# A cross network on one core: column tiles for the main matmuls, a second copy of the tail operand, a new load order, and a last layer with rows on partitions

## The chip, the cores and the metric

The kernel runs on one core of a Trainium2 chip. The metric is the device time of one execution in microseconds, the median of the runs; it was 140.9 us before the change (three runs, 139.42 to 141.42). The profile is one further execution, recorded by the hardware profiler; its span is 139.6 us. The engines are TensorE (PE; its weight loads are PEld), VectorE (DVE), ScalarE (ACT), GpSimd (POOL) and SyncE (SP), whose queue issues most DMAs. "Us" is microseconds everywhere.

## The reference

```
B, F, D, L = 4096, 26, 16, 6
Din = min(F * D, 1024)          # 416
# x0 [4096, 416], ws [6, 416, 416], bs [6, 416], all bf16
def reference(x0, ws, bs):
    x = x0
    for l in range(ws.shape[0]):
        x = x0 * (x @ ws[l] + bs[l]) + x
    return x
```

Six cross layers over 4096 rows of 416 features.

## The kernel before

Since every layer multiplies by `x0` and adds `x`, the state of layer l is x0 times a sum, S, that only grows: S after layer l is S before plus `x @ ws[l]` plus the bias. The kernel therefore keeps S in PSUM, lets TensorE accumulate into it through all six layers, and has another engine form `x = x0 * (S + bias)` from it. The biases are summed once over the layers (`cb_sb`, from a small matmul of a triangle of ones).

The features stand on partitions. The 416 features are three chunks of 128 (`NC = 3`) and a tail of 32 (`DR`). The 4096 rows are four blocks of 1024 columns (`NS = 4`, `SB = 1024`); a block goes through all six layers before the next. The tail of a block is packed: the four groups of 256 rows (`G`) lie on the four quadrants of 32 partitions, so the tail operand `xt_sb` is 128 x 256. PSUM has eight banks of 128 x 512 fp32: six hold S of the three chunks, one half bank (`TAIL`) S of the packed tail, another half (`SPARE`) the tail transposes of the next block.

TensorE runs, for each block and layer, in this order:

- `chunk(m, 0)`: the first half of the columns (512), as 18 matmuls of 128 x 128 weights and 256 columns (L263);
- the tail's rows into the three chunks: 12 matmuls whose contraction is the 32 tail features, tile shape 32 x 128, four row groups side by side (L312). They wait for the tail operand of this layer (`s_xt`) and for the second half's evictions (`s_xb`);
- the tail's outputs: 12 matmuls of 128 x 32 column tiles (L198), and four more with `wc_sb`, a block-diagonal copy of the 32 x 32 corner of the weights, for tail into tail;
- in layer 1, the transposes of the next block's tail (`tail_transposes`);
- `chunk(m, 1)`: the second half, 18 matmuls.

VectorE evicts a half as three 128 x 512 operations (L414): `x = (S + bias) * x0`, in bf16, into `xT_sb`, or into `xo_sb` after the last layer. ScalarE adds the bias to the tail (L457) into `t32_sb`, GpSimd multiplies it by the tail of x0 (L182) into `xt_sb` or, after the last layer, `xot_sb`. The corner copies into `wc_sb` are GpSimd's (L167): the first four after the layer-0 tail weights land, the others after the tail weights of layers 1 to 5 land.

A finished block is stored by SP's queue: three DMA transposes of `xo_sb` into `o_sb` (L129), one of `xot_sb` into `ot_sb` (L133), and, after GpSimd has moved `ot_sb` into the last 32 columns of `o_sb` (L190), one store (L136). GpSimd's part stands in its program behind the layer-1 product of the next block:

```
if l == 1 and s > 0:
    pool.wait_ge(s_ot, 16 * s)
    pool.tensor_copy(out=o_sb[...], in_=ot_sb[...]).then_inc(s_otc, 1)
```

The last block is not transposed by DMA: TensorE transposes it (L350, L364), VectorE and ScalarE copy it out of PSUM, and four stores follow.

At the start, the first 512 rows come in as rows and are transposed on TensorE (L225), the next 512 and the other blocks through transposing DMAs (L111, L121). SP's queue issues, in order: the first rows, weights of layer 0, the tail columns of rows 512 to 1023 (`xtl_sb`, L108), half of the layer-0 tail weights (the other half is ScalarE's queue), the transposing load of the first block's second half, weights of layer 1, tail weights of layers 1 to 5, weights of layers 2 to 5, the tail columns of the other blocks (L119), and the transposing loads of blocks 1 to 3. The order of all engines' programs is written out by hand with semaphores.

## Time and profile before

| What | Value |
|---|---|
| Median of three runs | 140.9 us (139.42 to 141.42) |
| Span of the profiled execution | 139.6 us, mean granted TensorE clock 0.981 |
| Chain that ended last | PE 83%, SP's queue 6%, DMA 5% |
| Main matmuls 128x256 (L263) | 864, 276 and 273 ns each, overlapping |
| Evictions 128x512 (L414) | 143, 744 ns each |
| Tail bias 128x256 (L457), tail product (L182) | 474 ns, 671 ns |
| Corner copies (L167) | 32x32 and 32x160, 201 to 321 ns |
| Output copy of the tail (L190) | 398 ns |
| Transposing stores: three of `xo_sb`, one of `ot_sb` | issued from 43.58, 73.83, 104.09; `ot_sb` from 48.74, 78.95, 108.13, landing 2.4 us after issue |

Rows of the profile give a line of the kernel, the engine, the operation, its output and inputs, shapes, and the mean length of one. [...] "Idle before" is the time the engine stood still ahead of an operation, and what ended it. An issue on SP's queue takes time on SP; the landing is counted from the issue.

### The profile page before, as it was taken

The page shows a single profiled execution, that of the slowest core. Times are in us where ns is not written, and L with a number is a line of the kernel's source. Part 1 is how long each engine was busy: PE and PEld are TensorE (multiplying, and loading weights), DVE is VectorE, ACT ScalarE, POOL GpSimd, SP SyncE. Part 2 cuts the span into 40 slices and gives each one's busy share as a digit, 9 for nine tenths or more (in the row PEclk, how much of TensorE's full clock was granted, in tenths as well). Part 3 has the DMA queues.
Part 4 walks back from the last instruction along what each step waited for, and adds up shares of the span by engine and source line. Part 5 has one row for each costly group of instructions (what it writes and reads, how often), then busy time and mean ns, then how long its engine had stood idle before and what let it go on. Part 6 is the DMA issues. An engine that isn't in the chain of part 4 may idle for free.

```text
span 139.6 us, 3659 instructions
## 1 busy us (share of the span) xinstructions
PE 129.5 (93%) x1638; PEld 102.3 (73%) x1638; DVE 98.5 (71%) x149; ACT 18.0 (13%) x38; POOL 22.3 (16%) x45
## 2 busy tenths in 40 slices
PE   6799389999999999999999999999999999999950
PEld 4677167877877887887787787787788788778730
DVE  0338505977977887897797797798779779779560
ACT  1510110110111021011011021001101101101370
POOL 5023400110110120111011021011011111101500
PEclk9999969999999999999999999999999999999997
DMA  4999799940004947000007934000008461000007
GB/s 132 229 249 315 114 229 227 129 97 5 0 0 39 116 97 249 0 0 5 0 0 43 189 105 161 0 5 0 0 5 159 90 206 38 5 0 0 5 3 244
DMA packets 32939, 12.17 MB, mean 87 GB/s; under 512 B 25238, under 2 KB 32924, under 8 KB 32924
## 3 DMA queue, kind: packets, MB, share of 16 engines
q1 hardware_dynamic: 32272, 11.45, 39.8%
q10 hardware_dynamic: 652, 0.48, 1.0%
q8 instruction: 13, 0.21, 0.7%
q14 instruction: 2, 0.02, 0.0%
HBM read 3.22 MB, written 3.41 MB: 47 GB/s over the span
## 4 chain that ended last, share of the span: by engine, by line
PE 83%; SPq 6%; DMA 5%; issue 1%; ACT 1%
PE ps L263 66%; PE ps L198 9%; PE ps L312 7%; DMA xtl_sb<-in_x_dram 5%; SPq L113 2%; SPq L116 1%; SPq L111 1%; SPq L110 1%; ACT o_sb L464 1%; PE ps L350 0%; SPq L108 0%; ACT o_sb L476 0%; SPq L106 0%; SPq L107 0%; ACT o_sb L469 0%
## 5 line engine op out<-in xcount | busy, mean ns | idle before, releaser
L414 DVE SCALAR_TENSOR_TENSOR xT_sb<-ps,cb_sb,x0T_sb 128x512 bf16<-128x512 f32 x120 | 81.1, 744 | 27.2 <-PE ps L312 24.0
L263 PE MATMUL ps<-xT_sb,w_sb 128*128 128x256 bf16 x720 | 84.4, 276 | 0.0
L263 PEld LDWEIGHTS ps<-xT_sb,w_sb 128*128 128x128 bf16 x720 | 69.7, 99 | 12.4 <-issue 3.6
L182 POOL TENSOR_TENSOR xt_sb<-t_sb,x0t_sb 128x256 bf16<-128x256 f32 x20 | 13.4, 671 | 85.6 <-ACT t_sb L457 85.6
L457 ACT ACTIVATE t_sb<-ps,cb_sb 128x256 f32<-128x256 f32 x24 | 11.4, 474 | 105.5 <-PE ps L198 105.5
L414 DVE SCALAR_TENSOR_TENSOR xo_sb<-ps,cb_sb,x0T_sb 128x512 bf16<-128x512 f32 x23 | 15.6, 744 | 4.5 <-PE ps L312 3.9
L263 PE MATMUL ps<-x0T_sb,w_sb 128*128 128x256 bf16 x144 | 17.1, 273 | 0.0
L263 PEld LDWEIGHTS ps<-x0T_sb,w_sb 128*128 128x128 bf16 x144 | 13.7, 98 | 2.5 <-issue 0.8
L312 PE MATMUL ps<-xt_sb,wt_sb 32*128 32x256 bf16 x240 | 10.1, 271 | 1.2 <-issue 1.2
L198 PE MATMUL ps<-xT_sb,w_sb 128*32 128x256 bf16 x240 | 10.2, 276 | 0.0
L312 PEld LDWEIGHTS ps<-xt_sb,wt_sb 32*128 32x128 bf16 x240 | 4.5, 92 | 5.6 <-issue 5.5
L198 PEld LDWEIGHTS ps<-xT_sb,w_sb 128*32 128x32 bf16 x240 | 4.6, 95 | 4.3 <-issue 4.2
L198 PE MATMUL ps<-xt_sb,wc_sb 128*32 128x256 bf16 x80 | 5.7, 273 | 0.0
L182 POOL TENSOR_TENSOR xot_sb<-t_sb,x0t_sb 128x256 bf16<-128x256 f32 x4 | 2.7, 672 | 13.1 <-ACT t_sb L457 13.1
L205 PE MATMUL ps<-ones_sb 128*128 128x256 bf16 x16 | 3.4, 391 | 1.2 <-POOL ones_sb L149 1.2
L394 DVE COPY x0T_sb<-ps 128x256 bf16<-128x256 bf16 x4 | 1.1, 291 | 4.6 <-PE ps L225 4.4
L205 PEld LDWEIGHTS ps<-ones_sb 128*128 128x128 bf16 x16 | 2.1, 139 | 1.9 <-POOL ones_sb L149 1.2
L167 POOL COPY wc_sb<-wt_sb 32x32 bf16<-32x32 bf16 (+1 forms) x8 | 2.1, 260 | 7.0 <-DMA wt_sb<-in_ws_dram 6.6
L198 PE MATMUL ps<-ident,xtl_sb 128*32 128x128 bf16 x28 | 1.2, 221 | 1.8 <-DMA xtl_sb<-in_x_dram 1.8
L198 PEld LDWEIGHTS ps<-ident,xtl_sb 128*32 128x32 bf16 x28 | 0.7, 96 | 2.1 <-DMA xtl_sb<-in_x_dram 2.1
L198 PEld LDWEIGHTS ps<-xt_sb,wc_sb 128*32 128x32 bf16 x80 | 2.1, 97 | 0.0
L198 PE MATMUL ps<-x0T_sb,w_sb 128*32 128x256 bf16 x48 | 2.0, 276 | 0.0
(35 smaller groups left out, 25.0 us busy)
## 6 DMA issues: line engine op xcount, KB each, us to landing
out_dram<-o_sb SPq DMA_DIRECT2D x3, 832.0 KB, 4.1
w_sb<-in_ws_dram SPq DMA_DIRECT2D x6, 312.0 KB, 6.6
out_dram<-o_sb SPq DMA_DIRECT2D x3, 208.0 KB, 2.3
wt_sb<-in_ws_dram SPq DMA_DIRECT2D x4, 130.0 KB, 4.5
xin_sb<-in_x_dram SPq DMA_DIRECT2D x1, 208.0 KB, 2.8
xin_sb<-in_x_dram ACTq DMA_DIRECT2D x1, 208.0 KB, 3.0
out_dram<-o_sb ACTq DMA_DIRECT2D x1, 208.0 KB, 2.6
xtl_sb<-in_x_dram SPq DMA_DIRECT2D x1, 192.0 KB, 7.6
```

What stands on the lines that cost most here:

```text
L110: sp.dma_start(wt_sb[32 * g:32 * g + 32, 0, :], ws[0, DF:D, :]).then_inc(s_wt[0], 16)
L111: sp.dma_start_transpose(x0T_sb[:, :, H:SB], x0[H:SB, 0:DF]).then_inc(s_x0T[0], 16)
L113: sp.dma_start(w_sb[:, l, :, :], wmain(l)).then_inc(s_w[l], 16)
L116: sp.dma_start(wt_sb[32 * g:32 * g + 32, 1:L, :], ws[1:L, DF:D, :].rearrange("l p n -> p l n")).then_inc(s_wt[1], 16)
L167: pool.tensor_copy(out=wc_sb[p, a:b, p], in_=wt_sb[p, a:b, DF:D]).then_inc(s_wc, 1)
L182: pool.tensor_tensor(out=dst, in0=t32_sb[:, n % 2, :], in1=x0t_sb[:, s, :], op=ALU.mult).then_inc(s_xt, 1)
L198: return pe.matmul(dst, lhsT=lhsT, rhs=rhs, start=start, stop=True, skip_group_check=True, tile_position=(0, 32 * q),)
L205: pe.matmul(ps[:, 7, 0:256], lhsT=ones_sb[:, 0:128], rhs=ones_sb[:, :], start=True, stop=True)
L263: ins = pe.matmul(ps[:, b, c:c + G], lhsT=w_sb[:, l, k, m * 128:(m + 1) * 128], rhs=src[:, k, off + g * G:off + (g + 1) * G], start=l == 0 ...
L312: ins = pe.matmul(ps[:, b, c:c + G], lhsT=wt_sb[p, l, m * 128:(m + 1) * 128], rhs=srct[p, :], start=l == 0 and g >= 2 and i < 2, stop=True ...
L414: dve.scalar_tensor_tensor(out=split(dst), in0=acc_half(c, half), scalar=cb_sb[:, c, l:l + 1], in1=split(x0T_sb[:, c, o:o + H]), op0=ALU.a ...
L457: act.activation(out=t32_sb[:, n % 2, :], in_=TAIL, func=ACTF.Identity, bias=cb_sb[:, NC, l:l + 1],).then_inc(s_ta, 1)
```

## The change

The engine programs are now recorded in one list through a small planner, `Plan.add`: each operation names what it reads, writes and accumulates into, and the waits are derived. The planner does not reorder: every engine runs its operations in the order of the calls. Its GpSimd copies that move data to other partitions (`shifts=True`) wait for the GpSimd operation ahead of them to end.

What differs in the work:

1. **Main matmuls.** Each 128 x 128 x 256 pair becomes four 128 x 32 column tiles of 512 columns, one PSUM bank for each half and chunk (`bank(h, m)`). 
2. **Tail.** The tail operand is held twice: `[:, 0]` as before, `[:, 1]` with neighbouring quadrants swapped (`swap`). Quadrants 0 and 2 then cover 512 columns in one row tile; quadrants 1 and 3 do it in two of 256. The corner, tail into tail, is done among the row tiles (with `wc_sb` in a new layout), and no longer among the column tiles. S of the tail lies in two half banks, so ScalarE's bias becomes two operations of 64 partitions. After GpSimd's product, two of the four swapped quadrants are copied by ScalarE and two by GpSimd; for the tail of x0 of a new block ScalarE copies all four, in layer 1 of the block before, ahead of that layer's bias.
3. **Loads.** See `load_...` below; the rows of the last block (`xr_sb`, 832 KB) are loaded as well. The ones are set by VectorE, and ScalarE runs a dummy activation first.
4. **Store of a block.** `store_block(s)` is called after a block's layers, so that GpSimd's copy (L450) stands directly behind the block's last product, ahead of the next block's first. SP waits chunk by chunk.
5. **Last layer of the last block.** Its output is made with rows on partitions: for each 128 rows, three matmuls of `x` against 416 columns of weights, three that bring in S so far (`sS_sb`, evicted by ScalarE) through the identity, and the tail likewise; VectorE (for two tiles ScalarE and GpSimd) multiplies by `xr_sb`, and five stores follow. The transposes on TensorE at the end are gone.

The core of the diff, with the lines that the prediction speaks of:

```
+        load_rows("sync", 0)
+        load_rows("scalar", 1)
+        load_main(0)
+        load("scalar", bsa_sb[1:L + 1, :], bs[:, :], "bs", [("bs",)])
+        load_transposed(0, H, SB)
+        load("sync", xtl_sb[:, 4:JS, :], x0_v[:, 4:JS, DF:D], "xtl0", [("xtl", 0)])
+        load_tail_weights(0, 1, "wt0")
+        load_main(1)
+        load_tail_weights(1, L, "wt1")
+        load_main(2)
+        load("sync", xtl_sb[:, JS:NJ, :], x0_v[:, JS:NJ, DF:D], "xtl1", [("xtl", 1)])
+        load_main(3)
+        load_main(4)
+        load_main(5)
+        for s in range(1, NS):
+            load_transposed(s, 0, SB)
+        load("sync", xr_sb[:, :, :], x0_v[:, (NS - 1) * JS:NJ, :], "xr", [("xr",)])
...
+        def main(s, l, h, m, k):
+                for q in range(4):
+                    f0 = m * 128 + 32 * q
+                    ins = mm(
+                        pe, ps[quad(q), bank(h, m), :], w_sb[:, l, k, f0:f0 + 32],
+                        src[:, k, off + h * H:off + (h + 1) * H], l == 0 and k == 0 and h == 0, (0, 32 * q),
+                    )
...
+        def tail_rows(s, l):
+            keys = [("wt", wkey(l)), key, key + ("swapped",)]
+            def rows(pe, q, h, m, start):
+                for part in range(2):
+                    if q % 2 == 0:
+                        if part:
+                            break
+                        dst, rhs = ps[:, bank(h, m), :], src[quad(q), :, :]
+                    else:
+                        dst, rhs = ps[:, bank(h, m), part * G:(part + 1) * G], src[quad(q), 1 - part, :]
+                    ins = mm(pe, dst, wt_sb[quad(q), l, m * 128:(m + 1) * 128], rhs, start and part == 0, (32 * q, 0))
...
+        def swap(tile, key, engines):
+            for g, eng in enumerate(engines):
+                dst, src = tile[quad(g), 1, :], tile[quad(g ^ 1), 0, :]
...
+        def leave_tail(s, l):
+            tail_halves(l, t, ("t32", l % 2))
+            P.add("gpsimd", lambda e: e.tensor_tensor(out=dst, in0=t, in1=x0t_sb[:, s, 0, :], op=ALU.mult), ...)
+            if l < L - 1:
+                swap(xt_sb[:, (l + 1) % 2], key, ("scalar", "gpsimd", "scalar", "gpsimd"))
...
+        def store_block(s):
+            for c in CH:
+                P.add("sync", lambda e, c=c: e.dma_start_transpose(o_sb[...], xo_sb[:, s, c, :]),
+                    reads=[("xo", s, c, h) for h in HALVES], writes=[("o", s)], dma="oT%d" % s)
+            P.add("sync", lambda e: e.dma_start_transpose(ot_sb[:, s, :, :], xot_sb[:, s, :]),
+                reads=[("xot", s)], writes=[("ot", s)], dma="ot%d" % s)
+            P.add("gpsimd", lambda e: e.tensor_copy(out=o_sb[...], in_=ot_sb[...]),
+                reads=[("ot", s)], writes=[("oc", s)])
+            P.add("sync", lambda e: e.dma_start(out_v[...], o_sb[...]),
+                reads=[("o", s), ("oc", s)], writes=[("out", s)], dma="out%d" % s)
...
+        for s in range(NS):
+            for l in range(L):
+                if s == NS - 1 and l == L - 1:
+                    break
...
+                    for m in CH:
+                        for k in CH:
+                            main(s, l, 0, m, k)
+                tail_rows(s, l)
+                for c in CH:
+                    leave(s, l, 0, c)
+                tail_outs(s, l)
+                if l == 1 and s < NS - 1:
+                    tail_in(s + 1)
+                leave_tail(s, l)
+                if s == 0 and l == 0:
+                    corner(1, L, "wt1")
+                if s == NS - 1 and l == L - 2:
+                    tail_halves(L - 1, st_sb, ("st",))
...
+            if s < NS - 1:
+                store_block(s)
...
+        for j in range(4):
+            row_main(j, True)
+            row_sums(j)
+        row_tails()
+        finish(0, None)
+        finish(1, 0)
+        finish(2, None)
+        finish(3, 1)
+        for j in range(4, 8):
+            row_main(j, False)
+            row_sums(j)
+            finish(j, None)
```

## The prediction

> **What bounds the kernel now.** I read the page first: busy times, and the granted clock in 40 slices.

> ```profile
> PE 129.5 (93%) x1638; PEld 102.3 (73%) x1638; DVE 98.5 (71%) x149; ACT 18.0 (13%) x38; POOL 22.3 (16%) x45
> ...
> PEclk9999969999999999999999999999999999999997
> ```

> TensorE is the bound (83% of the chain of waits is its own), and one early slice ran at a lower granted clock. Next the timelines of TensorE, SP's queue and GpSimd over a block boundary (start, length, engine, line, operation, idle before).

> ```profile
> 38.89 0.51 PE L312 MATMUL ps<-xt_sb,wt_sb 32*128 32x256 bf16 x12
> 39.32 0.51 PE L198 MATMUL ps<-xT_sb,w_sb 128*32 128x256 bf16 x12
> 39.66 0.28 PE L198 MATMUL ps<-xt_sb,wc_sb 128*32 128x256 bf16 x4
> 39.88 2.14 PE L263 MATMUL ps<-xT_sb,w_sb 128*128 128x256 bf16 x18
> 41.85 2.13 PE L263 MATMUL ps<-x0T_sb,w_sb 128*128 128x256 bf16 x18
> 43.91 0.51 PE L312 MATMUL ps<-x0t_sb,wt_sb 32*128 32x256 bf16 x12
> ```
> ```profile
> 43.58 5.12 SPq L129 DMA_TRANSPOSE o_sb<-xo_sb  x3
> 48.74 1.25 SPq L133 DMA_TRANSPOSE ot_sb<-xot_sb  x1
> ```
> ```profile
> 50.60 0.67 POOL L182 TENSOR_TENSOR xt_sb<-t_sb,x0t_sb 128x256 bf16<-128x256 f32 x1 [4.29 <-ACT t_sb L457]
> 51.23 0.40 POOL L190 COPY o_sb<-ot_sb 128x256 bf16<-128x256 bf16 x1
> ```

> A layer takes 43.91 - 38.89 = 5.02 us. Starts, not lengths, give the prices, since matmuls overlap. 18 full matmuls: 41.85 - 39.88 = 1.97, 0.109 each. Twelve column tiles: 39.66 - 39.32 = 0.34, so a round of four side by side takes 0.11, no more than one full matmul. The four corner tiles take 0.22: one round and 0.11 for the change of tile shape. Three shape changes per layer: 36 x 0.109 + 7 x 0.11 + 3 x 0.11 = 5.02. VectorE's six 744 ns evictions start 0.66 apart, 4.0 a layer, and hide.

> The copy of the tail's output (L190) waits for the `ot_sb` transpose, but stands behind the layer-1 product of the next block, so the wait cost nothing. Third, the head, first from TensorE's timeline, then busy time by windows of 3.41 us (the fields used are the PE busy time and the granted clock, the figure after the POOL count).

> ```profile
> 11.64 2.13 PE L263 MATMUL ps<-xT_sb,w_sb 128*128 128x256 bf16 x18
> 15.02 0.51 PE L312 MATMUL ps<-xt_sb,wt_sb 32*128 32x256 bf16 x12 [1.25 <-issue]
> ...
> 17.88 0.29 PE L198 MATMUL ps<-ident,xtl_sb 128*32 128x128 bf16 x8 [1.80 <-DMA xtl_sb<-in_x_dram]
> 18.11 5.77 PE L263 MATMUL ps<-xT_sb,w_sb 128*128 128x256 bf16 x36
> ```
> ```profile
> 11.37:14.78 3.41, 2.40 (x22) 1.90 (x20) 1.99 (x4) 0.00 (x0) 1.12 (x4) 1.00 1.16 320
> 14.78:18.19 3.41, 1.37 (x37) 0.80 (x38) 2.07 (x3) 0.47 (x1) 0.80 (x2) 1.00 0.57 74
> 18.19:21.61 3.42, 3.42 (x17) 2.46 (x18) 0.78 (x2) 0.38 (x1) 0.00 (x0) 0.50 1.14 247
> ```

> TensorE waits for corner weights (to 15.02), then for the `xtl_sb` load (to 17.88). The window with 1.37 us of work is followed by one at half clock, in which 36 matmuls take 5.77 instead of 4.10: 1.67 us lost. A window with 2.40 us of work was not punished. Last, ScalarE's end, with the last store:

> ```profile
> 134.83 0.39 ACT L469 ACTIVATE o_sb<-ps 128x256 bf16<-128x256 bf16 x1
> 135.09 0.89 ACT L476 ACTIVATE o_sb<-ps 128x512 bf16<-128x512 bf16 x2
> 136.02 0.48 ACTq L479 DMA_DIRECT2D out_dram<-o_sb  x1
> ```

> A 256-column ScalarE operation lasts 0.39 but frees the engine after 135.09 - 134.83 = 0.26.

> The sum is made against the span, 139.6. Nothing of note lies around it: the runs shown go from 139.42 to 141.42, so the median of 140.9 stands 1.3 above the span.

> **The layer.** The 36 full matmuls become 18 rounds of four 512-column tiles. By the rows a round costs what its columns cost: 2 x 0.109 less one start overhead, 0.216; 18 x 0.216 = 3.89. Column outputs drop from four rounds to three (0.33), the shape changes from three to two (0.2): both halves and the outputs now have one shape. The tail rows mix one 512-column tile with two of 256 on neighbouring row groups. If they run fully side by side, two times 0.216 = 0.43. TensorE's records start in program order, and the second 256-column tile must wait for the first on its row group, so everything behind it waits too: five slots of 0.11, 0.56. I take 0.56, nearest to the in-order rows. Layer: 3.89 + 0.33 + 0.2 + 0.56 = 4.98 (4.85 with overlap), a gain of 0.05 (0.18) over some 20 layers: -1.0 (bound -3.5).

> [...]

> VectorE keeps its 4.0 per layer inside 4.98; its last eviction of a second half ends about 1.65 into the next layer, ahead of the tail rows at 2.05.

> **The second tail copy.** Call the start of a layer's first-half matmuls zero. First half 1.95, shape change to 2.05, rows to 2.61, outputs 2.7 to 3.04, second half to 4.98. ScalarE's bias in two halves starts at 3.26 (as now, 0.33 after the last output round) and ends at 4.0 (0.47 and one spacing of 0.27); GpSimd's product 0.67, to 4.76; then two copies each on ScalarE and GpSimd. A 32x256 GpSimd copy, bounded by the corner copies (0.2 at 32 columns, 0.31 at 160) and the 128x256 copy (0.40): 0.39, with its own wait 0.45, twice: 5.66. The next rows need it at 4.98 + 2.05 = 7.03: hidden with 1.3 to spare. In layer 1 of blocks 0 to 2, ScalarE first does the next block's tail copy and four shifts (0.38 + 4 x 0.27 = 1.5), so the chain ends near 7.3: 0.2 late, twice outside the head: +0.4.

> **The moved copy.** On GpSimd the output copy (now L450, waiting for the `ot` transpose) stands directly behind the block's last product. Queued behind it are the next block's layer-0 product (L432) and shifts (L398); for those TensorE's layer-1 tail rows wait, and behind these everything. From the next block's zero: VectorE's eviction of chunk 0's second half ends at 0.35, SP starts at 0.44 (it now waits per chunk, some 1.3 earlier than now). By the rows the `ot` transpose follows 48.74 - 43.58 = 5.16 later, at 5.6 (third boundary: 104.09 to 108.13, 4.04), and lands 2.4 after its issue: 8.0. Copy 0.4, product 0.67, two copies 0.9, waits 0.1: 10.1. The rows want it at 7.03. Stall 3.1, 3.1 and 2.0 = +8.2 (bounds 6.0 with the short spacing everywhere; 9.3 with the long).

> Such a gap lies within a window of 3.41 or is cut by two. A gap of 3.1 leaves one window with 0.3 to 1.9 us of work; 1.37 was punished, 2.40 not. I count two half-clock windows of 1.67 over the three boundaries: +3.3 (bounds 0 and 5.0). [...]

> **The head.** The transposing load moves up past two loads, so `wt_sb` for layer 0 is issued last on SP at about 5.6 instead of 2.9 and lands (4.0) near 9.3; corner copies 4 x 0.27 follow to 10.4, and the layer-0 tail rows wait for these instead of starting at 8.67. Then: outputs and second half to 13.2, layer 1's first half to 15.2, its corner weights (landing 13.4 now, up to 1 later, then 1.5 of copies) at about 15.6, outputs to 16.3, second half to 18.4, layer 2's first half to 20.4. The `xtl_sb` load goes from 10.19 to about 9.05, before three weight loads instead of behind them: landed before TensorE asks at 16.3. With the 0.2 of the late chain layer 2's rows start near 20.7 instead of 23.81: -3.1; -1.4 if a window drops there too, -4 if the loads are early. The moved ones memset and the ScalarE table load hide behind the loads; the added 832 KB row load stands last on SP, 100 us ahead of its use.

> **The last layer.** From layer 4's zero now: 122.6 to 139.6, 17.0. After: row tile 0 needs a bank that ScalarE frees by its second tail bias, behind the shifts, at 5.85: stall 1.0. The identity sums need three 128x512 evictions of ScalarE (starts 0.48 apart, 0.69 long): 7.85, stall 1.3. Eight row tiles of 3 x 0.176 + 3 x 0.057 = 0.70, tails 0.65: the last ends at 13.55. VectorE's 128x416 product, about 0.65, to 14.45; issue, landing and end 2.9 (now 139.6 - 136.02 = 3.6 for twice the bytes): 17.3. +0.3 (bounds -0.5; +2 with a dropped window).

> **Sum.** 139.6 - 1.0 + 0.4 + 8.2 + 3.3 - 3.1 + 0.3 = 147.7. Half of the 1.3 between span and median added: 148.3.

> **Rivals.** (a) The stalls come without clock drops: 145.0. For it: a gap may be cut in two by the window's edge. Against: 1.37 of work was punished. 0.12. (b) Rows overlap fully, the short spacing holds at every boundary, no drop: 147.7 - 2.5 - 2.2 - 3.3 = 139.7, some 140.5 as a median: no change. 0.14. (c) Faster: the `ot` transpose lands by 4.9 from the block's zero, so that copy, product and shifts fit ahead of 7.03. Then 8.2 and 3.3 vanish: 136.2, as a median 137. It decides at 4.9 against 8.0 by the rows (6.9 at the third boundary); only an earlier start speaks for it, and that is counted. 0.09. (d) Head and end drop a window as well: 147.7 + 1.7 + 1.7 = 151.1. Waits of 1.0 and 1.3 within 3 us at the end speak for it. 0.17. The forecast has 0.48.

> **Numbers.** Faster by over 2% is below 138.1, slower above 143.7, about what a measurement of this kernel can tell. Slower: forecast, (a) and (d), 0.77; same (b) 0.14; faster (c) 0.09. The range from 141.5 to 152.5 leaves out (c), most of (b) and a little above (d).

> **What would show it.** Three gaps of 2 to 3 us on TensorE ahead of layer 1's tail rows in blocks 1 to 3, with GpSimd idle until the `ot` transpose lands; half-clock windows behind two of them; layers of 4.85 to 5.0 elsewhere; the `xtl_sb` wait gone. The prediction is wrong if the copy starts within 5 us of a block's start, or if column rounds of 512 take clearly more than 0.216.

## The result and the profile after

The changed kernel takes 148.13 us (median of four executions, 146.27 to 150.67) against 140.26 before (four, 139.42 to 141.42). The ratio is 1.045, 95% interval 1.034 to 1.056; it compares only the executions of each kernel that lie near its fastest, here 146.27 and 147.16, so it lies below the ratio of the medians. The prediction was 148.3. The profiled execution has a span of 147.9 (before 139.6), and all readings below are of it.

How many half-clock windows an execution holds varies. The mean granted clock of the four is 0.965 (the profiled one), 0.954, 0.987 and 0.988, at spans of 147.9, 149.4, 145.9 and 145.0. A window of 3.41 us at half clock, as the trace shows them below, lowers the mean by 3.41 x 0.5 / 147.9 = 0.0115; by this estimate the four hold three, four, one and one such windows. The windows below are those of the profiled execution.

TensorE's work did not grow: its busy time, in which half-clock windows count in full (3.41 us busy of 3.41 in the one below), is 129.2 us, before 129.5. The granted clock in 40 slices, from the page, shows three dips where the kernel before has one, early in its run:

```profile
PEclk9999999999999689999999779999999869999999
```

The timeline of TensorE over the second block boundary (start, length, engine, line, operation, idle before):

```profile
70.54 0.60 PE L258 MATMUL ps<-xt_sb,wt_sb 32*128 32x512 bf16 x7
...
75.42 0.60 PE L258 MATMUL ps<-x0t_sb,wt_sb 32*128 32x512 bf16 x7
75.65 0.27 PE L258 MATMUL ps<-x0t_sb,wc_sb 32*128 32x256 bf16 x1
75.66 0.37 PE L258 MATMUL ps<-x0t_sb,wt_sb 32*128 32x512 bf16 x1
75.66 0.38 PE L258 MATMUL ps<-x0t_sb,wc_sb 32*128 32x256 bf16 x3
75.97 2.46 PE L258 MATMUL ps<-x0T_sb,w_sb 128*32 128x256 bf16 x48
78.25 2.12 PE L258 MATMUL ps<-xT_sb,w_sb 128*32 128x512 bf16 x36
82.28 0.59 PE L258 MATMUL ps<-xt_sb,wt_sb 32*128 32x512 bf16 x7 [1.91 <-POOL xt_sb L398]
```

A layer without a wait takes 75.42 - 70.54 = 4.88 (before 5.02). From the second half's first matmul to the next layer's, 78.25 - 75.97 = 2.28 holds three output rounds and nine rounds of 512 columns: (2.28 - 0.33) / 9 = 0.217 a round. Then, in layer 1 of the next block, the tail rows stand 1.91 us for GpSimd. GpSimd and SP's queue at that place:

```profile
80.20 0.40 POOL L450 COPY o_sb<-ot_sb 128x256 bf16<-128x256 bf16 x1 [6.84 <-DMA ot_sb<-xot_sb]
80.56 0.67 POOL L432 TENSOR_TENSOR xt_sb<-t_sb,x0t_sb 128x256 bf16<-128x256 f32 x1
81.29 0.84 POOL L398 COPY xt_sb<-xt_sb 32x256 bf16<-32x256 bf16 x2
```
```profile
73.76 4.00 SPq L441 DMA_TRANSPOSE o_sb<-xo_sb  x3
77.80 1.25 SPq L446 DMA_TRANSPOSE ot_sb<-xot_sb  x1
```

GpSimd idles for 6.84 us in front of the copy, whose transpose is issued last of four, at 77.80, and lands 2.35 later; product and shifts follow without a pause, and TensorE starts 0.15 after the last shift. The three gaps are 3.64, 1.91 and 2.77: 8.3 us together. The work of TensorE in the clock's windows of 3.41 us around this gap (PE busy first; the granted clock is the figure after the POOL count):

```profile
79.84:83.25 3.41, 1.50 (x44) 0.81 (x40) 0.61 (x2) 0.83 (x2) 1.81 (x4) 1.00 0.51 173
83.25:86.66 3.41, 3.41 (x44) 1.41 (x40) 2.84 (x5) 2.97 (x7) 0.00 (x0) 0.50 0.26 82
```

The window with the gap holds 1.50 us of work, and the next one runs at half clock. In this execution there are three such windows, one per boundary; each makes its stretch 1.67 longer (72 matmuls in 5.73 instead of 4.06 behind this gap), 5.0 us together. Head and end, from TensorE's timeline:

```profile
15.74 0.30 PE L258 MATMUL ps<-ident,xtl_sb 128*32 128x128 bf16 x8 [0.54 <-DMA xtl_sb<-in_x_dram]
...
20.91 0.59 PE L258 MATMUL ps<-xt_sb,wt_sb 32*128 32x512 bf16 x7 [1.00 <-ACT xt_sb L396]
...
136.81 0.69 PE L258 MATMUL ps<-w_sb,xT_sb 128*128 128x416 bf16 x3 [1.31 <-ACT st_sb L419]
139.07 0.34 PE L258 MATMUL ps<-ident,sS_sb 128*128 128x128 bf16 x3 [1.57 <-ACT sS_sb L549]
```

The balance against before, from marks that both kernels have: layer 2's tail rows of block 0 start at 20.91 instead of 23.81 (-2.9); from there to layer 4's tail rows of the last block, 132.50 - 20.91 = 111.6 instead of 124.54 - 23.81 = 100.7 (+10.9); from there to the end 15.4 instead of 15.1 (+0.3). The middle part is 8.3 + 5.0 + 0.2 (a late chain) - 20 x 0.14 = 10.7.

### The profile page after: what moved, and what is told of

Read it like the earlier page. It is cut to its first block, busy times and chain, and to the rows that moved or that the text cites. A ratio compares the mean times of both kernels' runs of the same rounds, so it can differ in the third digit from the quotient of the medians.

```text
span 147.9 us, 5168 instructions
## 1 busy us (share of the span) xinstructions
PE 129.2 (87%) x2352; PEld 65.7 (44%) x2352; DVE 98.5 (67%) x149; ACT 52.7 (36%) x117; POOL 38.5 (26%) x84
## 3 DMA queue, kind: packets, MB, share of 16 engines
HBM read 4.07 MB, written 3.41 MB: 51 GB/s over the span
## 4 chain that ended last, share of the span: by engine, by line
PE 62%; DMA 10%; ACT 7%; SPq 7%; POOL 6%; DVE 4%; issue 3%
PE ps L258 62%; DMA ot_sb<-xot_sb 6%; DMA xtl_sb<-in_x_dram 4%; SPq L186 4%; DVE xT_sb L409 3%; POOL xt_sb L432 3%; ACT x0t_sb L396 2%; POOL xt_sb L398 2%; ACT t_sb L419 2%; SPq L204 1%; ACT xt_sb L396 1%; SPq L441 1%; ACT sS_sb L549 1%; POOL o_sb L450 1%; ACT x0t_sb L387 1%
## 5 line engine op out<-in xcount | busy, mean ns | idle before, releaser
L258 PE MATMUL ps<-xT_sb,w_sb 128*32 128x512 bf16 (+1 forms) x1596 | 89.2, 378 | 0.0
L258 PEld LDWEIGHTS ps<-xT_sb,w_sb 128*32 128x32 bf16 x1596 | 42.1, 100 | 40.5 <-issue 9.2
L419 ACT ACTIVATE t_sb<-ps,cb_sb 64x256 f32<-64x256 f32 x46 | 21.6, 469 | 48.4 <-PE ps L258 48.1
L432 POOL TENSOR_TENSOR xt_sb<-t_sb,x0t_sb 128x256 bf16<-128x256 f32 x20 | 13.4, 670 | 58.1 <-ACT t_sb L419 58.1
L396 ACT ACTIVATE xt_sb<-xt_sb 32x256 bf16<-32x256 bf16 x40 | 16.6, 414 | 27.5 <-POOL xt_sb L432 27.2
L258 PE MATMUL ps<-xt_sb,wt_sb 32*128 32x512 bf16 (+1 forms) x152 | 12.2, 334 | 9.6 <-POOL xt_sb L398 8.5
L258 PE MATMUL ps<-x0T_sb,w_sb 128*32 128x512 bf16 (+1 forms) x336 | 18.5, 365 | 0.2 <-DVE x0T_sb L485 0.2
L398 POOL COPY xt_sb<-xt_sb 32x256 bf16<-32x256 bf16 x40 | 15.7, 392 | 2.5
L258 PEld LDWEIGHTS ps<-x0T_sb,w_sb 128*32 128x32 bf16 x336 | 8.4, 97 | 7.7 <-issue 0.8
L258 PE MATMUL ps<-xt_sb,wc_sb 32*128 32x256 bf16 x76 | 7.6, 276 | 0.0
L450 POOL COPY o_sb<-ot_sb 128x256 bf16<-128x256 bf16 x3 | 1.2, 396 | 23.1 <-DMA ot_sb<-xot_sb 23.1
L258 PE MATMUL ps<-w_sb,xT_sb 128*128 128x416 bf16 x24 | 5.5, 339 | 1.3 <-ACT st_sb L419 1.3
L432 POOL TENSOR_TENSOR xot_sb<-t_sb,x0t_sb 128x256 bf16<-128x256 f32 x3 | 2.0, 671 | 9.9 <-ACT t_sb L419 9.9
```

The source lines that it names most:

```text
L258: return pe.matmul(dst, lhsT=lhsT, rhs=rhs, start=start, stop=True, skip_group_check=True, tile_position=pos,)
L396: fn = lambda e, d=dst, s=src: e.activation(out=d, in_=s, func=ACTF.Copy)
L398: fn = lambda e, d=dst, s=src: e.tensor_copy(out=d, in_=s)
L419: "scalar", lambda e, p=p, h=h: e.activation(out=dst[p, :], in_=ps[p, T_BANK[h], 0:G], func=ACTF.Identity, bias=cb_sb[p, NC, l:l + 1]), re ...
L432: "gpsimd", lambda e: e.tensor_tensor(out=dst, in0=t, in1=x0t_sb[:, s, 0, :], op=ALU.mult),
L450: "gpsimd", lambda e: e.tensor_copy(out=o_sb[:, s * JS:(s + 1) * JS, DF:D].rearrange("p (g r) f -> p r g f", r=2), in_=ot_sb[:, s, :, :].r ...
```

## The experiments

Spans are those of one profiled execution each; a median and a ratio to the kernel before stand beside them. One thing must be taken out in comparing spans: in the profiled executions of copy_later, gap_filled, ot_first and full_tiles (granted clocks 0.986, 0.988, 0.987 and 0.987) a half-clock window falls into the end as well, where TensorE has two waits (1.31, in full_tiles 1.18, and 1.57). In copy_later, from the last layer's first matmul to the end is 138.1 - 125.71 = 12.4, in the changed kernel without such a window 147.9 - 136.81 = 11.1: 1.3 us.

**copy_later.** The edit, with the function `store_block` cut in two:

```
         def store_block(s):
             ...                                          # the four transposes on SP
+
+        def store_block_end(s):
             P.add("gpsimd", ... tensor_copy o_sb <- ot_sb ...)
             P.add("sync", ... dma_start out_v <- o_sb ...)
...
                 leave_tail(s, l)
+                if l == 1 and s > 0:
+                    store_block_end(s - 1)
```

> One edit to the changed kernel: GpSimd's copy of the tail's output (and the store behind it) is recorded behind layer 1's tail product of the next block instead of directly behind the block's last product; loads, tiles and the last layer stay. Theory (the copy's wait for the ot_sb transpose holds up the next block's first product): the three gaps ahead of layer 1's tail rows (3.64, 1.91, 2.77 = 8.3 us) and the three half-clock windows behind them (1.67 each = 5.0 us) both vanish, 147.9 - 13.3 = 134.6; without the slow windows layer 2's rows of blocks 1 and 2 will wait about 1 us each for ScalarE's four shifts, as block 0's do now, so 136 to 137. Rival (column tiles and the second tail copy cost the time, the gaps are a symptom of late DMA): the transposes still land as late, the gap stays or moves to another instruction, 145 or more.

Measured: span 138.1, median 138.22 (137.39 to 139.42), ratio 0.981, interval 0.966 to 0.996. Without the window at the end 136.8; two other executions, with a granted clock of 1.0 throughout, have spans of 136.1 and 136.3. GpSimd at the first boundary:

```profile
43.03 0.68 POOL L432 TENSOR_TENSOR xt_sb<-t_sb,x0t_sb 128x256 bf16<-128x256 f32 x1 [4.20 <-ACT t_sb L419]
...
51.79 0.40 POOL L452 COPY o_sb<-ot_sb 128x256 bf16<-128x256 bf16 x1
```

The layer-0 product no longer waits, the copy finds its data landed, no gap and no half-clock window is left at a boundary, and layer 2's rows wait 1.05 in blocks 1 and 2. One copy's place on GpSimd accounts for the whole loss.

**ot_first.** The transpose of the tail's output moves to the head of SP's four; the copy stays where the change put it.

```
         def store_block(s):
+            P.add("sync", ... dma_start_transpose ot_sb <- xot_sb ...)
             for c in CH:
                 P.add("sync", ... dma_start_transpose o_sb <- xo_sb ...)
-            P.add("sync", ... dma_start_transpose ot_sb <- xot_sb ...)
```

> One edit to the changed kernel: SP issues the ot_sb transpose ahead of the three xo_sb transposes of a block; GpSimd's copy keeps its place ahead of the next block's product. Theory: the tail's output is ready about 0.3 us ahead of the next block, so the transpose lands about 2.5 us into it, before the product's input is there (about 4): gaps and half-clock windows vanish as in copy_later, 136 to 137. Rival (the place of the copy on GpSimd costs by itself, or the transposes interfere with TensorE's operands whenever they run): gaps of 2 us or more remain, 142 or more.

Measured: span 137.9, median 139.21 (137.57 to 139.37), ratio 0.987, interval 0.974 to 1.000, so as fast as the kernel before or a little faster. GpSimd at the first boundary:

```profile
40.78 0.40 POOL L450 COPY o_sb<-ot_sb 128x256 bf16<-128x256 bf16 x1 [2.39 <-DMA ot_sb<-xot_sb]
42.59 0.67 POOL L432 TENSOR_TENSOR xt_sb<-t_sb,x0t_sb 128x256 bf16<-128x256 f32 x1 [1.41 <-ACT t_sb L419]
```

The copy still waits 2.39 for the transpose, but is done before ScalarE delivers the product's input. No gap is left at the boundaries. So the place of the copy costs nothing by itself: the loss needs both the copy's place ahead of the product and a transpose that lands late.

**gap_filled.** TensorE works through the gap instead of standing still; the results of this work are not read.

```
+                if l == 1 and s > 0:
+                    gap(34)      # 34 matmuls of ones, 128x32 weights, 256 columns
                 tail_rows(s, l)
```

> One edit to the changed kernel: ahead of layer 1's tail rows of blocks 1 to 3 TensorE runs 34 matmuls of ones into unused columns of a PSUM bank (34 x 0.109 = 3.7 us), which none of the results read. The wait for GpSimd stays. Theory (the half-clock windows come from the gaps): the gaps filled with work, no half-clock window in the three boundaries, 5.0 us less, but the fill outlasts the two shorter gaps by 1.8 and 0.9: 147.9 - 5.0 + 2.7 = 145 to 146. Rival (the lower clock has another cause, such as the column tiles' load): three windows at half clock remain and the fill only adds, 149 to 151.

Measured: span 149.4, median 150.42 (150.12 to 150.71), ratio 1.069, interval 1.059 to 1.080. The granted clock in 40 slices, from the page, is

```profile
PEclk9999999999999999999999999999999999999699
```

The first 37 slices, up to 138.2, all have 0.9 or more: the three half-clock windows at the boundaries are gone. All four executions have a granted clock of 0.987 to 0.989, about one window each. So the theory holds for the clock, but the time was expected 3.5 to 4.5 lower and came out where the rival had it. The fill was counted rightly. Taken from the start of layer 1's first half, less the 2.05 that a first half takes (75.42 - 73.37 in the changed kernel), the tail rows come 3.9, 3.7 and 3.7 late, where the gaps made them 3.7, 2.0 and 2.8 late: +2.8. What was not counted: layer 2's rows wait 1.05 in two blocks where a half-clock window had hidden it (0.21 and nothing, +1.9); the end has a window of its own (149.4 - 136.77 = 12.6 against 11.1, +1.5); and the head is 0.2 longer (layer 2's rows at 21.12 instead of 20.91). 147.9 - 5.0 + 2.8 + 1.9 + 1.5 + 0.2 = 149.3.

**full_tiles.** copy_later with the main matmuls as before, in `main`:

```
-                for q in range(4):      # 128x32 weights, 512 columns, tile (0, 32 q)
+                for g in range(2):      # 128x128 weights, 256 columns
```

> The copy_later kernel with the main matmuls as before the change: 128x128 weights, two of 256 columns in place of four 128x32 tiles of 512. Theory (a column round costs what its columns cost, the gain is start overheads and one change of tile shape): a layer goes from 4.88 to about 5.0, 0.12 x 20 = 2.4 us more than copy_later. Rival (512-column tiles save nothing or cost): same as copy_later within 0.5 us, or faster.

Measured: span 140.7, median 141.79 (140.27 to 142.72), ratio 1.007, interval 1.001 to 1.013. Both spans have the window at the end: +2.6 over copy_later. A layer, from its tail rows to those of the next, takes 67.47 - 62.44 = 5.03 against 4.88. The column tiles do gain, 0.15 a layer.

**old_loads.** copy_later with the loads in the order before the change.

```
-        load_transposed(0, H, SB)       # now third on SP; back behind xtl0 and half of wt0
-        load("sync", xtl_sb[:, JS:NJ, :], ...)    # now behind load_main(2); back behind load_main(5)
```

> The copy_later kernel with the loads issued in the order before the change (xtl_sb and the layer-0 tail weights ahead of the transposing load, half of these weights on ScalarE's queue, the other blocks' xtl_sb behind all weights). Theory (the head's gain is the load order): TensorE waits again for xtl_sb until about 17.9, layer 2's rows of block 0 start near 23.5 instead of 20.9, 2.5 to 3 us more than copy_later, with a half-clock window in the head. Rival (the head's gain came from the layer, not from the loads): within 1 us of copy_later.

Measured: span 138.0, median 140.44 (139.28 to 141.77), ratio 0.989, interval 0.978 to 1.000. TensorE waits for the tail columns again:

```profile
17.44 0.29 PE L260 MATMUL ps<-ident,xtl_sb 128*32 128x128 bf16 x8 [2.21 <-DMA xtl_sb<-in_x_dram]
```

Layer 2's rows start at 22.63 against 21.37 in copy_later, 1.3 later, not 2.5 to 3: the wait came back, the half-clock window did not. Its window, 15.44 to 18.85, holds 1.41 us of work. So the load order is worth 1.3 here, and more only where a window falls. The profiled execution has a granted clock of 1.0 throughout; the other three have 0.976 to 0.988, so windows fell in them, but no trace shows where.

**shift_later.** copy_later, and ScalarE's part of `tail_in(s + 1)` recorded behind `leave_tail`:

```
                 if l == 1 and s < NS - 1:
-                    tail_in(s + 1)       # transposes, ScalarE's copy and four shifts
+                    tail_in(s + 1)       # transposes
                 leave_tail(s, l)
+                if l == 1 and s < NS - 1:
+                    tail_in_act(s + 1)   # ScalarE's copy and four shifts
```

> The copy_later kernel with ScalarE's copy and four shifts of the next block's tail behind its own layer-1 bias and shifts, where before they stood ahead of them. Theory: layer 2's rows no longer wait in blocks 0 to 2, about 1 us each, 3 us less than copy_later. Rival: another input of these rows is as late; within 0.5 us of copy_later.

Measured: span 133.1, median 135.01 (134.24 to 137.65), ratio 0.953, interval 0.941 to 0.965. The waits of 1.00, 1.05 and 1.05 at layer 2 are gone; against 136.8 the span is 3.7 lower, 0.6 more than these waits, with an uneven head (in copy_later 1.1 us of waiting for the corner at 15.5, here none). Between the executions with a granted clock of 1.0, spans of 133.0 and 133.1 here and 136.1 and 136.3 there, it is 3.0 to 3.3, the sum of the waits.

**no_dead_shift.** copy_later without shifts that nothing reads:

```
-            if l < L - 1:
+            if l < L - 1 and not (s == NS - 1 and l == L - 2):
                 swap(...)
```

> The copy_later kernel without the four shifts of the tail operand for the last layer of the last block, which that layer does not read. Theory (the end waits for ScalarE, whose second tail bias stands behind these shifts): the bias starts 1.6 us earlier, and the last layer's first matmul and sums with it: 1.3 to 1.6 us less than copy_later. Rival (the end is bound by the evictions of the last second half or by VectorE): less than 0.5 us.

Measured: span 134.8, median 136.26 (136.08 to 136.74), ratio 0.963, interval 0.955 to 0.970. From layer 4's rows in the last block to the end is 134.8 - 121.08 = 13.7, in the changed kernel 15.4: 1.7 less. The first wait is gone, the one for the evictions of S (1.33) remains.

**all_three.** copy_later, shift_later, no_dead_shift together, and one more edit:

```
         for j in range(4):
             row_main(j, True)
-            row_sums(j)
+        for j in range(4):
+            row_sums(j)
```

> The changed kernel with the copy behind layer 1's product, and three more edits: ScalarE's copy and four shifts of the next block's tail stand behind its own layer-1 bias and shifts; the shifts of layer 4 of the last block, which the last layer does not read, are left out; the first four row tiles of the last layer run their x matmuls before the identity sums. Theory: copy_later (136.5), less about 1 us at layer 2 of each of blocks 0 to 2, less the 1.6 us by which ScalarE's second tail bias starts earlier, less about 1 us at the end where the sums wait behind four tiles of matmuls instead of one: 130 to 132. Rival (these waits were hidden by others, the sum is bound by TensorE already): within 1 us of copy_later.

Measured: span 130.8, median 132.01 (131.49 to 132.08), ratio 0.938, interval 0.929 to 0.947: faster than both kernels. Behind the first 10 us TensorE waits 0.6 us in all.

**probe_copies.** all_three with 24 ScalarE copies that nothing reads. The question was the 0.42 us between ScalarE's shifts, where the prediction had 0.27.

> The all_three kernel with six groups of four ScalarE copies of 256 bf16 columns into a scratch tile that nothing reads, each group in a stretch where ScalarE stands idle: on 128 partitions; on the first 32; on each 32 in place; on each 32 into its neighbour's partitions; on 64; on 96. Measured are the starts within a group. Before the change a ScalarE operation on 128 partitions freed the engine after 0.26 of its 0.39; the changed kernel's shifts of 32 partitions start 0.42 apart at 0.41 long. Theory A (an operation on fewer than 128 partitions does not overlap the next): 0.26 in the first group, about 0.42 in all others. Theory B (the move to other partitions stops the overlap): 0.26 in all groups but the fourth. Theory C (reading from SBUF instead of PSUM does it): 0.4 in all six. The time is that of all_three, 131 to 132.

Measured: span 130.6, one run of 131.83. ScalarE's timeline; three of the six groups:

```profile
23.48 1.33 ACT L477 ACTIVATE scr_sb<-ones_sb 128x256 bf16<-128x256 bf16 x4
...
28.36 1.33 ACT L477 ACTIVATE scr_sb<-ones_sb 32x256 bf16<-32x256 bf16 x4
...
33.25 1.69 ACT L477 ACTIVATE scr_sb<-ones_sb 32x256 bf16<-32x256 bf16 x4
```

These are four copies on all partitions, four on partitions 0 to 31, four on one quadrant each, in place. Starts are 0.31 apart in the first two groups and 0.43 in the third; 64 and 96 partitions give 0.31, the move to the neighbour's partitions 0.43. All three theories fall: neither fewer partitions, nor the move, nor SBUF does it. What the two groups with 0.43 share is that each operation begins at another partition than the one before. That it is the change, and not a start away from partition 0, is seen at the first copy, which follows two shifts (22.62, 0.84 long): it goes back to partition 0 and still starts (23.48) only behind the end of the second shift (22.62 + 0.84 = 23.46). Why the overlapping groups have 0.31 and not the 0.26 of the kernel before stays open.

## Why the prediction was right, and where its terms were off

- **The wait taken over by GpSimd's copy.** Right in mechanism, place and size: 8.3 against 8.2. copy_later removes it from GpSimd's side, ot_first from SP's. The single gaps were 3.64, 1.91 and 2.77 where 3.1, 3.1 and 2.0 were said: the long spacing of SP's transposes does not fall on the same boundary each time (4.1, 4.0 and 4.9 from the first to the fourth), and at the first the last transpose took 4.0 to land.
- **The clock.** Right in mechanism, mis-sized in the profiled execution: 5.0 instead of 3.3, three windows instead of two. The prediction let one gap escape by its place in the windows; here none did, down to the one that left 1.50 us of work. By the granted clocks the four executions hold about three, four, one and one, so two was a fair middle; one kernel had one to four. gap_filled shows that the gaps cause the windows at the boundaries.
- **The layer.** Mis-sized: 0.14 gained per layer instead of 0.05, so -2.8 instead of -1.0 over 20 layers. The step that failed is the tail rows in five slots of 0.11 (0.56), which took their tiles to start in program order; here they did not (see the last section). The profile shows 0.23 from 75.42 to 75.65 for the first six tiles, and the whole in about 0.45 (75.97 - 75.42, less 0.1 for the change of tile shape): the prediction's lower bound of 0.43, side by side. Its own terms gave 5.02 - 4.98 = 0.04, written as 0.05. The rounds (0.217 against 0.216) were right, though no run shows the start overhead of 0.002 in them apart, and full_tiles confirms their worth.
- **The second tail copy in layer 1.** Mis-sized: 1.0 late in blocks 0 to 2, not 0.2. ScalarE's shifts start 0.42 apart, not 0.27, and the two halves of the bias 0.48: probe_copies shows what the shifts' spacing depends on. In the changed kernel's profiled execution the half-clock windows hide most of it (0.21 in block 1, nothing in block 2), so it cost little there; shift_later shows it in full. It also means that a half-clock window there costs less than its 1.67 in the end.
- **The head.** -2.9 against -3.1. The tail weights landed at 7.9, earlier than the 9.3 said (its own terms, 5.6 and 4.0, give 9.6), and the shifts made layer 2 wait 1.0, later than said. The `xtl_sb` wait was not gone but 0.54. old_loads puts 1.3 us of the gain on the load order; that the window of before would always be saved with it isn't shown.
- **The end.** +0.3 as said, but by terms that cancel: the waits are 1.31 and 1.57 where 1.0 and 1.3 were counted, and TensorE's last matmul ends some 0.9 later than said; the rest behind it takes 3.0 instead of 3.75. That no window fell here was chance: in four experiments one did.

The sum was closer than its terms: in the profiled execution the clock was put 1.7 too low and the layer's gain 1.8 too low, and the two cancel. That the median lies within 0.2 of 148.3 is luck as well: it is the middle between 147.16 and 149.11, an execution with about one half-clock window and one with three.

## What to carry to other kernels

When a program is recorded in the order of calls, an instruction that waits for a DMA goes where its data has landed, not where it belongs by subject: everything behind it on its engine inherits the wait (here GpSimd's product and shifts, behind 6.84 us of idling at the second boundary). Read a moved wait by what is queued behind it and by the latest landing in the trace, and add the lower clock that may follow a gap (1.67 us behind each of the three here, nothing behind the 2.21 in old_loads). The gain of 0.14 us per layer was real all along; one copy in the wrong place cost about 9 to 11 us (147.9 to 136.8 between the profiled executions, without the end's own window; 145.0 and 145.9 to 136.1 and 136.3 between those with the fewest half-clock windows), and waits behind ScalarE's shifts and some dead work 6 more (136.8 to 130.8); without them 4.5% slower became 6% faster.
